# An earlier start for the feed-forward groups, two homes for their input, and an earlier switch of the cycle's form

## The chip, the core and the metric

The kernel runs on one core of one Trainium2 chip. Its engines work side by side and each takes its own instructions in order: TensorE (PE; its weight loads are shown apart as PEld), VectorE (DVE), ScalarE (ACT), GpSimd (POOL) and SyncE (SP), which issues the DMAs. The metric is the device time of one launch in microseconds, median of several runs; lower is better. TensorE's clock has two levels, 2.4 and 1.2 GHz; the profile shows the granted clock as 1.00 and 0.50.

## The reference

Attention over 64 heads (8 batches of 8 heads, 576 tokens, head size 64), in which scores more than tau below their row's maximum are dropped, and then a feed-forward layer over all 4608 tokens:

```python
scores = q @ k^T / sqrt(64)
thresh = max(scores) - tau
scores = where(scores >= thresh, scores, -1e9)
attn   = exp(scores - max) / (sum + 1e-9)
x = (attn @ v), heads side by side           # 4608 x 512
h = x @ w_in                                 # 512 x 2048
out = (max(h, 0) + alpha * min(h, 0)) @ w_out
```

## The kernel before

Two heads of a batch make a pair (32 pairs, 4 a batch, the class `Pair`). A pair has nine **units** (128 query rows of one head each, and one mixed unit at position 4). Most products are made from a high and a low part of each operand, three matmuls for one.

The main loop runs over **cycles** i from -3 to 297; unit i belongs to pair i // 9 at position i % 9, and the last unit is 287 (`total` = 288). The order of the instructions on TensorE, ScalarE, VectorE and GpSimd is the order in which this loop writes them down. In cycle i it masks unit i (L475, VectorE), makes the scores of unit i + 2 (L440, TensorE), turns unit i (L484 and L500, transposes on TensorE), then runs what tables hold for this cycle (`soon`, then `later`; `at_cycle` and `first_at_cycle` fill them), copies the turned unit (L536, ScalarE, high part; one cycle on L540, VectorE, low part) and takes a later unit's row maximum (L455, VectorE) and exponential with its threshold (L463 and L468, ScalarE). There are two score buffers, so scores of unit i + 2 wait for the mask of unit i.

The cycle has two **forms**. While i < SW (`ab`), maxima and exponentials are made two in each odd cycle and none in an even one, and the low part's place alternates; from SW on each cycle takes the low part of unit i - 1 right behind the scores and the maximum and exponential of unit i + 2 at its end. SW is 52.

The tables hold for each pair: products with v (L587) at positions 5, 6, 1 and 2, their copies out (L598, L600, ScalarE) one cycle on; the high part of the next pairs' keys `kh` (L367, ScalarE) and the low part `kl` (L374, GpSimd) at position 7; scaled queries (L387, L392) at position 0; and the pair's closing steps, the last of which (`fin_out`, L647) stores the pair's x (`xs`) to DRAM in position 7 of the next pair's turn. The first four pairs (one batch) are worked in whole 32-bit form and close one cycle later (cycle 44 for the batch).

The **feed-forward work** for the first seven of sixteen blocks of d_ff fills TensorE between attention's matmuls (class `Mlp`). Tokens go in 18 groups of 256. A group is ready RDY cycles behind the 36 units of the batch that holds its last token. For a group: `load_x` (one DMA, L206, into `xr`), `split_x` (xh on ScalarE, L212; xl on GpSimd, L214), seven chunks of layer 1 (`step_l1`, 12 matmuls each, L226), each followed by the activation (L238 VectorE, L239 ScalarE, L249 GpSimd) and its own split (L255, L256, GpSimd), then 42 matmuls of layer 2 (`step_l2`, L262), whose two sums are copied out by ScalarE (`po`, L768) and stored as `part`. `Mlp.cycle` holds a budget in assumed microseconds (`room`): each cycle adds CYCLE less what attention uses in it, a chunk costs 1.31 and a matmul of layer 2 costs 0.216; no chunk goes into the cycles with products with v, and at most GB = 11 chunks' results are kept. The x of a group stands in the same queue as its chunks, as an item of its own:

```python
if self.l1 and i >= self.gap and self.live < GB:
    if self.l1[0][2] is None:
        self.step_l1(i)          # load; split at i + XO; self.gap = i + XO + 2
    elif slot and self.room > TH1 and ...:
        l1 = True                # one chunk in this cycle
```

`xr`, `xh` and `xl` have one buffer each, so a group's x is loaded once the last chunk of the group before is out, and its first chunk follows three cycles later (XO = 1).

Behind the loop what is left of the queue is drained (`jobs`, `first_layer`, `second_layer`, x by `fetch_x`), and then the other nine blocks of d_ff are worked with a product scheme of seven multiplications (L1319 to L1612).

SyncE's DMAs are not in the hand-written order; the framework places them.

Of the kernel before, what the change touches and what calls it, by code (L numbers as in the profile page):

```python
# [11 lines left out]
F32R = mybir.dt.float32r  # L12
# [9 lines left out]
P = 128  # L22
D = 64
S = 576
NKC = 4
F1 = 7
G1 = 256
# [9 lines left out]
GB = 11  # L37
# [2 lines left out]
CLOSE = 10  # L40
DEC2, DEC3 = 5, 6
L2S = 7
SW = 52
THR = 'a'
QLV = 0
SPG = 'p'
# [4 lines left out]
FINS = (9, 11, 12, 12, 15, 16, 16)  # L51
ACTO, SPLO, PUTO = 1, 2, 1
TH1, TH2, TH3 = 0.75, -0.45, 0.1
XO = 1
L2O = 3
P1 = 2
LD = 12
# [3 lines left out]
EVD = lambda i: EVP[i % len(EVP)]  # L61
DEC0, DEC = -3, 3
DECO0, DECO = 16, 3
RDY = 13
CYCLE = 2.6
EW0, EW1, EW2 = (0, 1, 2, 3, 3, 3, 6), (0, 1, 2, 5, 6, 6, 7), (0, 1, 5, 6, 6, 7, 7)
EW = (
# [21 lines left out]
def tile_masked_attention_moe(  # L89
# [11 lines left out]
    nc = tc.nc  # L101
    B, NPAIR = q.shape[0], q.shape[1]
    NT, DM = out.shape
    NCC = DM // P
# [17 lines left out]
    groups1 = [(t, min(G1, NT - t)) for t in range(0, NT, G1)]  # L122
# [70 lines left out]
    ready = set()  # L193
# [504 lines left out]
    class Mlp:  # L698


        def __init__(self):
            self.l1, self.l2 = deque(), deque()
            self.acc = None
            self.live = 0
            self.gap = 0
            self.room = 0.0

        def ready(self, gi):
            t0, n = groups1[gi]
            st = {"g": {}}  # L710
            self.l1.append((gi, st, None))
            for i in range(F1):
                self.l1.append((gi, st, i))

        def step_l1(self, i):
            gi, st, fi = self.l1.popleft()
            t0, n = groups1[gi]
            if fi is None:
                st["xr"] = load_x(mem.mp1, t0, n, G1, 1)
                (at_cycle if i < total else first_at_cycle)(i + XO, lambda: st.update(x=split_x(mem.mp1, st["xr"], t0, n, G1, 1, nc.vector if i >= total else None)))  # L720
                self.gap = i + XO + 2
                return
            name = f"a{gi}_{fi}"
            self.live += 1
            ph = layer1(ps_m, fcs1[fi], n, st["x"], name)

            alone = i >= total

            def act(ph=ph):
                if alone:  # L730
                    st[fi] = (prelu(mem.mp1, G1, fcs1[fi], n, ph, name, 2),)
                    return
                st[fi] = prelu1(mem.mp1, G1, fcs1[fi], n, ph, name, 2)
                prelu2(*st[fi], n)

            def spl():
                g = mem.mp1.tile([P, 2, G1], F32R, tag="g", name=f"g{name}", bufs=GB)
                split_g(g, st.pop(fi)[0], n, None if alone else dict(p=nc.gpsimd, v=nc.vector).get(SPG))
                st["g"][fi] = g

            if alone:
                first_at_cycle(i + ACTO, act)
                first_at_cycle(i + SPLO, spl)
            else:
                at_cycle(i + ACTO, act)
                at_cycle(i + SPLO, spl)
            if fi == F1 - 1:
                for o in range(0, n, P):
                    for fj in range(F1):
                        self.l2.extend((i + L2O, gi, st, o, fj, ti) for ti in range(3))  # L750
# [22 lines left out]
        def cycle(self, i, used, slot):  # L773

            self.room = min(self.room, TH3) + CYCLE - used
            l1 = False
            if self.l1 and i >= self.gap and self.live < GB:
                if self.l1[0][2] is None:
                    self.step_l1(i)
                elif slot and self.room > TH1 and ("i", fcs1[self.l1[0][2]]) in ready:  # L780
                    l1 = True
                    self.room -= 1.31
            while self.l2 and self.l2[0][0] <= i and self.l2[0][4] in self.l2[0][2]["g"] and ("o", fcs1[self.l2[0][4]]) in ready and self.room > TH2:
                self.step_l2(i)
                self.room -= 0.216
            return l1
# [104 lines left out]
    def fetch_x(t0, n, c, lead, name, home):  # L891

        st = {}

        def load(k):
            if k == 0:
                st["parts"] = tuple(home.tile([P, NCC, G1], F32R, tag=t, name=f"{t}{name}", bufs=1) for t in ("xh", "xl"))
            xl = f(st["parts"][1])
            t = t0
            while t < t0 + n:  # L900
                b, o = divmod(t, S)
                m = min(S - o, t0 + n - t)
                nc.sync.dma_start(xl[:, k, t - t0 : t - t0 + m], xs[b][k, :, o : o + m])
                t += m

        def split(k):
            xh, xl = st["parts"]
            nc.scalar.activation(xh[:, k, :n], f(xl[:, k, :n]), AF.Copy)
            nc.gpsimd.tensor_tensor(xl[:, k, :n], f(xl[:, k, :n]), f(xh[:, k, :n]), op=ALU.subtract)
            if k == NCC - 1:  # L910
                st["x"] = st["parts"]

        for k in range(NCC):
            at_cycle(c, load, k)
            at_cycle(c + lead + k // 2, split, k)
        return st
# [4 lines left out]
    with tc.manual_schedule(engines=ENGINES) if ENGINES else ExitStack():  # L921
# [12 lines left out]
        for i in range(-3, total + CLOSE):  # L934
# [14 lines left out]
                do(i + 1, "expo")  # L949
            do(i, "turn")  # L950
            do(i, "turn_k")
            while nready < len(groups1) and sum(groups1[nready]) <= (i - RDY) // (9 * NPAIR) * S:
                mlp.ready(nready)
                nready += 1
            used = 0.92
# [747 lines left out]
```

## Time and profile before

| | |
|---|---|
| median of 3 runs | 1350.35 us (1349.82 to 1351.16) |
| profiled execution | 1351.17 us, its span 1349.4 us |
| mean granted clock of TensorE | 0.994 |
| busy | PE 1303.7 us, DVE 1133.0, ACT 957.9, POOL 773.3 |
| chain that ended last | PE 79%, DVE 8%, ACT 6%, DMA 3% |

The span is the time from the first to the last instruction; the rest of an execution's time lies around it. A row of a stretch gives the busy time of each engine in it, with the number of instructions; matmuls' ends are modelled, so a run of matmuls shows about 0.2 us more busy time than their starts lie apart. "Idle before" is the time for which an engine stood still ahead of an instruction, with what ended it.

### The profile page before, as it was taken

What the parts mean: (1) busy time and instruction counts of PE and PEld (TensorE: products, weight loads), DVE (VectorE), ACT (ScalarE), POOL (GpSimd) and SP (SyncE); (2) the same over time, 40 slices, a digit from 0 to 9 for tenths busy, and PEclk for the clock granted to TensorE, in tenths of its full rate; (3) what the DMA queues carried; (4) which work ended last, traced back from release to release, by engine and by line L of the source; (5) the groups of instructions that cost most, each with busy time, mean ns of one, the idle gap of its engine ahead of it and who ended that gap; (6) DMA issues with size and microseconds to landing.
All of it is one profiled execution on the core that took longest, in us unless ns stands there. A gap on an engine that the chain in (4) does not pass through costs nothing.

```text
span 1349.4 us, 26387 instructions
## 1 busy us (share of the span) xinstructions
PE 1303.7 (97%) x9052; PEld 1224.2 (91%) x9052; DVE 1133.0 (84%) x2150; ACT 957.9 (71%) x2103; POOL 773.3 (57%) x945
## 2 busy tenths in 40 slices
PE   5998899999999999999999999999999999999999
PEld 4556789999999999999999999889999999999999
DVE  6999888888888888988988987686788877977876
ACT  6888888888888888888888886254666666433332
POOL 4887476676576576666666654485888875000000
PEclk9999899999999999999999999999999999999999
DMA  8654544544554544454544533722566437766641
GB/s 258 165 153 115 150 128 113 162 132 121 148 142 125 141 138 136 135 140 136 141 134 136 139 89 112 248 66 87 186 191 188 161 109 254 247 197 190 201 134 70
DMA packets 140006, 202.98 MB, mean 150 GB/s; under 512 B 16000, under 2 KB 84640, under 8 KB 139872
## 3 DMA queue, kind: packets, MB, share of 16 engines
q1 hardware_dynamic: 139872, 201.29, 50.6%
q8 instruction: 72, 1.18, 0.4%
q14 instruction: 62, 0.51, 0.1%
HBM read 108.08 MB, written 51.00 MB: 118 GB/s over the span
## 4 chain that ended last, share of the span: by engine, by line
PE 79%; DVE 8%; ACT 6%; DMA 3%; issue 2%; POOL 1%; SPq 1%; ACTq 0%; DVEq 0%; POOLq 0%
PE av L587 11%; PE s L440 11%; PE pha L226 10%; PE acca L262 9%; PE t L484 8%; PE pX L1576 7%; PE pX L1319 6%; PE pW L1576 4%; PE pW L1319 3%; PE pY L1576 2%; PE pO L1337 2%; PE pY L1319 1%; PE accj L262 1%; DVE p L475 1%; PE tk L500 1%
## 5 line engine op out<-in xcount | busy, mean ns | idle before, releaser
L455 DVE TENSOR_REDUCE nmx<-s 128x1 f32<-128x576 f32 x288 | 217.3, 754 | 73.5 <-PE s L440 70.3
L475 DVE SCALAR_TENSOR_TENSOR p<-s,thr,p 128x576 f32<-128x576 f32 x256 | 207.0, 809 | 2.8 <-ACT thr L468 2.4
L463 ACT ACTIVATE p<-s,nmx 128x576 f32<-128x576 f32 x256 | 190.2, 743 | 6.6 <-DVE nmx L455 6.3
L262 PE MATMUL acca<-wo,ga 128*128 128x512 f32 x588 | 186.1, 423 | 0.8 <-issue 0.8
L440 PE MATMUL s<-kh,qst 128*128 128x288 f32 x640 | 142.1, 312 | 33.9 <-DVE p L475 21.1
L226 PE MATMUL pha<-xh,wi 128*128 128x256 f32 x792 | 158.5, 283 | 0.2 <-ACT pra L239 0.2
L484 PE MATMUL t<-ident,p 128*128 128x128 f32 x1024 | 155.1, 274 | 0.0
L440 PEld LDWEIGHTS s<-kh,qst 128*128 128x128 f32 x640 | 101.1, 192 | 57.5 <-issue 28.3
L440 PE MATMUL s<-kl,qst 128*128 128x288 f32 x640 | 134.2, 300 | 0.0
L226 PEld LDWEIGHTS pha<-xh,wi 128*128 128x128 f32 x792 | 129.0, 190 | 4.7 <-ACT pra L239 1.8
L484 PEld LDWEIGHTS t<-ident,p 128*128 128x128 f32 x1024 | 127.2, 142 | 0.1
L262 PEld LDWEIGHTS acca<-wo,ga 128*128 128x128 f32 x588 | 102.0, 191 | 12.5 <-issue 1.2
L226 PE MATMUL pha<-xl,wi 128*128 128x256 f32 x396 | 111.7, 282 | 1.3 <-DVE xl L214 1.3
L249 POOL TENSOR_TENSOR pta<-pta,pra 128x256 f32<-128x256 f32 x94 | 69.3, 737 | 74.0 <-ACT pra L239 69.8
L1319 PE MATMUL pX<-xh,wa 128*128 128x384 f32 x384 | 106.4, 337 | 1.0 <-DVE pZ L1392 0.5
L587 PE MATMUL av<-eo,vst 128*128 128x322 f32 (+1 forms) x512 | 107.3, 333 | 0.0
L540 DVE TENSOR_TENSOR eo<-t,eo 128x512 fp32r<-128x512 f32 (+1 forms) x168 | 97.4, 592 | 8.3 <-ACT eo L536 8.2
L440 PEld LDWEIGHTS s<-kl,qst 128*128 128x128 f32 x640 | 102.7, 192 | 0.0
L886 ACT ACTIVATE gh<-gr 128x1024 fp32r<-128x1024 f32 x45 | 47.7, 1060 | 76.8 <-PE pX L1576 32.5
L1576 PE MATMUL pX<-wb,gh 128*128 128x256 f32 x560 | 101.5, 283 | 0.0
L536 ACT ACTIVATE eo<-t 128x512 fp32r<-128x512 f32 (+1 forms) x168 | 84.6, 521 | 5.1 <-PE t L484 4.3
L1576 PEld LDWEIGHTS pX<-wb,gh 128*128 128x128 f32 x560 | 87.1, 191 | 0.0
(250 smaller groups left out, 3906.4 us busy)
## 6 DMA issues: line engine op xcount, KB each, us to landing
gd<-c SPq DMA_DIRECT2D x72, 192.0 KB
gr<-gd SPq DMA_DIRECT2D x24, 512.0 KB
kr<-in_k_dram SPq DMA_DIRECT2D x31, 320.0 KB
rb<-rvd SPq DMA_DIRECT2D x64, 144.0 KB
xs<-xa SPq DMA_DIRECT2D x32, 288.0 KB
pin<-part SPq DMA_DIRECT2D x18, 512.0 KB
vr<-in_v_dram SPq DMA_DIRECT2D x28, 320.0 KB
qr<-in_q_dram SPq DMA_DIRECT2D x31, 288.0 KB
```

Source lines behind the costliest of these rows:

```text
L226: nc.tensor.matmul(ph[:, :n], w[:, c, :], xx[:, c, :n], start=(c == 0 and ti == 0), stop=(c == NCC - 1 and ti == 2),)
L262: nc.tensor.matmul(acc[:m, :], gg[:, g, o : o + m], w, start=(first and ti == 0), stop=(last and ti == 2))
L440: nc.tensor.matmul(ps[:, h, :288], w, kk[:, a + h * 288 : a + (h + 1) * 288], start=(ki == 0 and i == 0), stop=(ki == 1 and i == n - 1),)
L455: nc.vector.tensor_reduce(self.nmx[:, j : j + 1], self.S[u][0][:, :, :288], axis=AX.XY, op=ALU.max, negate=True)
L463: nc.scalar.activation(pj, ps[:, :, :288], AF.Exp, bias=nmx[:, j : j + 1], scale=1.0)
L475: nc.vector.scalar_tensor_tensor(pj, ps[:, :, :288], thr[:, j : j + 1], pj, op0=ALU.is_ge, op1=ALU.mult, accum_out=self.sm[:, c : c + 1])
L484: nc.tensor.transpose(tb[:, c, :], pt[:, j, j * D + c * P : j * D + (c + 1) * P], ident)
L536: nc.scalar.activation(dst[0], ps, AF.Copy)
L540: nc.vector.tensor_tensor(dst[1], ps, f(dst[0]), op=ALU.subtract)
L587: nc.tensor.matmul(pa[:m, :n], w, x, start=(part == 0 and c == 0), stop=(part == z.parts[-1] and c == NKC))
L1319: nc.tensor.matmul(ph[:, :H1], a, x[:, c], start=(fresh and c == 0 and ti == 0), stop=(c == 1 and ti == 2), skip_group_check=not fresh,)
L1576: nc.tensor.matmul(acc[:, tb * H2 : (tb + 1) * H2], g[:, pr, tb * P : (tb + 1) * P], w, start=(fresh and (pr if final else n) == 0 and ti ...
```

## The change

- SW goes from 52 to 44: cycles 44 to 51 have the later form.
- RDY goes from 13 to 9: a group is ready four cycles sooner. Groups are no longer made ready behind the last unit.
- A group's x leaves the queue of chunks and gets a queue of its own (`xq`, `step_x`). It is loaded when at most XL = 2 chunks of the groups with a loaded x are left; its split follows XO = 2 cycles later (it was 1), and its chunks may go from the fourth cycle after the load on (`at`).
- `xh` and `xl` get two buffers each in the pool of the loop (also where `fetch_x` uses that pool).

```diff
@@ -40,7 +40,7 @@
 CLOSE = 10
 DEC2, DEC3 = 5, 6
 L2S = 7
-SW = 52
+SW = 44
 THR = 'a'
 QLV = 0
 SPG = 'p'
@@ -51,7 +51,8 @@
 FINS = (9, 11, 12, 12, 15, 16, 16)
 ACTO, SPLO, PUTO = 1, 2, 1
 TH1, TH2, TH3 = 0.75, -0.45, 0.1
-XO = 1
+XO = 2
+XL = 2
 L2O = 3
 P1 = 2
 LD = 12
@@ -61,7 +62,7 @@
 EVD = lambda i: EVP[i % len(EVP)]
 DEC0, DEC = -3, 3
 DECO0, DECO = 16, 3
-RDY = 13
+RDY = 9
 CYCLE = 2.6
 EW0, EW1, EW2 = (0, 1, 2, 3, 3, 3, 6), (0, 1, 2, 5, 6, 6, 7), (0, 1, 5, 6, 6, 7, 7)
 EW = (
@@ -699,27 +700,28 @@
 
 
         def __init__(self):
-            self.l1, self.l2 = deque(), deque()
+            self.l1, self.l2, self.xq = deque(), deque(), deque()
             self.acc = None
             self.live = 0
-            self.gap = 0
             self.room = 0.0
 
         def ready(self, gi):
             t0, n = groups1[gi]
             st = {"g": {}}
-            self.l1.append((gi, st, None))
+            self.xq.append((gi, st))
             for i in range(F1):
                 self.l1.append((gi, st, i))
+
+        def step_x(self, i):
+            gi, st = self.xq.popleft()
+            t0, n = groups1[gi]
+            st["xr"] = load_x(mem.mp1, t0, n, G1, 1)
+            (at_cycle if i < total else first_at_cycle)(i + XO, lambda: st.update(x=split_x(mem.mp1, st["xr"], t0, n, G1, 2, nc.vector if i >= total else None)))
+            st["at"] = i + XO + 2
 
         def step_l1(self, i):
             gi, st, fi = self.l1.popleft()
             t0, n = groups1[gi]
-            if fi is None:
-                st["xr"] = load_x(mem.mp1, t0, n, G1, 1)
-                (at_cycle if i < total else first_at_cycle)(i + XO, lambda: st.update(x=split_x(mem.mp1, st["xr"], t0, n, G1, 1, nc.vector if i >= total else None)))
-                self.gap = i + XO + 2
-                return
             name = f"a{gi}_{fi}"
             self.live += 1
             ph = layer1(ps_m, fcs1[fi], n, st["x"], name)
@@ -774,10 +776,10 @@
 
             self.room = min(self.room, TH3) + CYCLE - used
             l1 = False
-            if self.l1 and i >= self.gap and self.live < GB:
-                if self.l1[0][2] is None:
-                    self.step_l1(i)
-                elif slot and self.room > TH1 and ("i", fcs1[self.l1[0][2]]) in ready:
+            if self.xq and len(self.l1) - F1 * len(self.xq) <= XL:
+                self.step_x(i)
+            if self.l1 and i >= self.l1[0][1].get("at", i + 1) and self.live < GB:
+                if slot and self.room > TH1 and ("i", fcs1[self.l1[0][2]]) in ready:
                     l1 = True
                     self.room -= 1.31
             while self.l2 and self.l2[0][0] <= i and self.l2[0][4] in self.l2[0][2]["g"] and ("o", fcs1[self.l2[0][4]]) in ready and self.room > TH2:
@@ -894,7 +896,7 @@
 
         def load(k):
             if k == 0:
-                st["parts"] = tuple(home.tile([P, NCC, G1], F32R, tag=t, name=f"{t}{name}", bufs=1) for t in ("xh", "xl"))
+                st["parts"] = tuple(home.tile([P, NCC, G1], F32R, tag=t, name=f"{t}{name}", bufs=2 if home is mem.mp1 else 1) for t in ("xh", "xl"))
             xl = f(st["parts"][1])
             t = t0
             while t < t0 + n:
@@ -949,7 +951,7 @@
                 do(i + 1, "expo")
             do(i, "turn")
             do(i, "turn_k")
-            while nready < len(groups1) and sum(groups1[nready]) <= (i - RDY) // (9 * NPAIR) * S:
+            while i < total and nready < len(groups1) and sum(groups1[nready]) <= (i - RDY) // (9 * NPAIR) * S:
                 mlp.ready(nready)
                 nready += 1
             used = 0.92
```

## Rows read from the trace of the kernel before

**Rows 1.** The page, first part: busy time of an engine, share of the span, instructions.

```profile
PE 1303.7 (97%) x9052; PEld 1224.2 (91%) x9052; DVE 1133.0 (84%) x2150; ACT 957.9 (71%) x2103; POOL 773.3 (57%) x945
```

**Rows 2.** Stretches from the start of cycle 52 to that of 122 and on to 830 us. Columns here and in all rows of stretches: start:end and length in us; busy us (instructions) of PE, PEld, DVE, ACT, POOL; granted TensorE clock; share of the DMA engines; GB/s.

```profile
161.20:357.78 196.58, 193.15 (x1417) 183.65 (x1416) 173.81 (x387) 168.97 (x405) 129.83 (x166) 1.00 0.50 136
357.78:830.00 472.22, 470.96 (x3438) 448.35 (x3437) 414.50 (x918) 405.13 (x962) 307.73 (x388) 1.00 0.48 134
```

**Rows 3.** The chain that ended last, 900 to 925 us: start, length, what. Six chunks of layer 1 and 42 matmuls of layer 2.

```profile
904.15 8.82 PE phj L226 x72
912.98 9.52 PE accj L262 x42
```

**Rows 4.** Stretches of cycles 44, 45, 46, 47, of 48 to 51 together, and of 50 alone.

```profile
137.10:139.17 2.07, 1.31 (x9) 1.10 (x10) 1.66 (x4) 1.79 (x5) 2.07 (x3) 1.00 0.60 133
139.17:142.31 3.14, 1.20 (x8) 1.00 (x9) 2.96 (x8) 2.53 (x6) 0.73 (x2) 0.89 0.84 191
142.31:146.61 4.30, 4.30 (x20) 4.28 (x21) 3.17 (x6) 2.57 (x7) 1.19 (x1) 0.50 0.88 239
146.61:150.46 3.85, 3.85 (x24) 3.79 (x24) 1.75 (x4) 2.07 (x5) 0.00 (x0) 0.76 0.91 237
...
150.46:161.20 10.74, 8.82 (x58) 8.52 (x56) 9.11 (x22) 9.62 (x25) 7.26 (x8) 0.84 0.26 69
...
154.86:158.55 3.69, 3.69 (x19) 3.67 (x20) 3.10 (x8) 3.34 (x7) 2.47 (x2) 0.56 0.48 144
```

**Rows 5.** Stretches of cycles 54, 55, 56, of 57 to 60 together, of 59, and of 63, 64, 65.

```profile
166.36:169.58 3.22, 2.66 (x20) 2.48 (x21) 3.19 (x9) 3.13 (x8) 2.03 (x4) 1.00 0.92 263
169.58:171.93 2.35, 2.35 (x19) 2.28 (x20) 2.35 (x6) 1.56 (x5) 2.27 (x4) 1.00 0.64 169
171.93:175.05 3.12, 3.12 (x25) 3.06 (x24) 2.50 (x6) 2.65 (x7) 1.69 (x3) 1.00 0.74 189
...
175.05:185.59 10.54, 10.11 (x81) 9.88 (x80) 9.75 (x24) 9.18 (x26) 8.50 (x13) 1.00 0.22 58
...
180.18:182.94 2.76, 2.33 (x21) 2.12 (x19) 2.75 (x9) 2.03 (x6) 2.68 (x4) 1.00 0.29 70
...
190.75:194.04 3.29, 1.23 (x8) 1.02 (x9) 3.26 (x9) 3.20 (x8) 2.08 (x4) 1.00 0.92 263
194.04:196.48 2.44, 2.44 (x20) 2.31 (x20) 2.10 (x6) 2.22 (x5) 2.36 (x4) 1.00 0.69 172
196.48:200.03 3.55, 3.55 (x27) 3.40 (x26) 2.75 (x6) 2.66 (x7) 2.12 (x1) 1.00 0.67 167
```

**Rows 6.** Stretches of cycles 80 and 81.

```profile
239.44:242.22 2.78, 2.78 (x24) 2.68 (x23) 2.78 (x7) 2.37 (x8) 2.13 (x4) 1.00 0.89 235
242.22:245.05 2.83, 2.83 (x19) 2.46 (x17) 2.79 (x8) 2.74 (x7) 1.57 (x3) 1.00 0.88 255
```

**Rows 7.** ScalarE's timeline in cycle 205 (position 7): start, length, engine, line, operation, out<-in. `kh` of a coming pair, the turned unit's high part, and the exponential of the unit two on.

```profile
592.62 0.74 ACT L367 ACTIVATE kh<-kr 128x640 fp32r<-128x640 f32 x1
593.39 0.60 ACT L536 ACTIVATE eo<-t 128x512 fp32r<-128x512 f32 x1
593.88 0.73 ACT L463 ACTIVATE p<-s,nmx 128x576 f32<-128x576 f32 x1
```

**Rows 8.** The timelines of VectorE and TensorE behind it: low part, max, mask with the reading of its sum, and the scores that wait for the mask; then the same end of a mask and the scores behind it in cycle 210.

```profile
594.02 0.69 DVE L540 TENSOR_TENSOR eo<-t,eo 128x512 fp32r<-128x512 f32 x1 [0.27 <-ACT eo L536]
...
595.12 0.76 DVE L455 TENSOR_REDUCE nmx<-s 128x1 f32<-128x576 f32 x1
595.80 0.81 DVE L475 SCALAR_TENSOR_TENSOR p<-s,thr,p 128x576 f32<-128x576 f32 x1
596.53 0.08 DVE L475 DVE_READ_ACCUMULATOR p<-s,thr,p 128x1 f32 x1
...
597.13 0.42 PE L440 MATMUL s<-kh,qst 128*128 128x288 f32 x2
...
605.41 0.08 DVE L475 DVE_READ_ACCUMULATOR p<-s,thr,p 128x1 f32 x1
...
605.75 0.51 PE L440 MATMUL s<-kh,qst 128*128 128x288 f32 x2
```

**Rows 9.** The split of x on ScalarE (all 15; ns min/median/max), and stretches of three cycles with the same work at position 3: 201 without a split in the cycle before, 210 and 138 with one.

```profile
L212 ACT ACTIVATE xh<-xr x15: 1047/1061/1066, 155.7 to 842.2; 128x1024 fp32r<-128x1024 f32 x15
...
580.50:583.15 2.65, 2.65 (x17) 2.27 (x16) 2.18 (x6) 2.41 (x7) 1.20 (x5) 1.00 0.27 96
605.75:608.61 2.86, 2.77 (x17) 2.27 (x16) 2.44 (x6) 2.70 (x8) 2.54 (x6) 1.00 0.02 6
402.94:406.17 3.23, 2.78 (x18) 2.32 (x17) 2.97 (x6) 3.19 (x10) 2.91 (x6) 1.00 0.41 149
```

**Rows 10.** TensorE's timeline behind the loop: the two waits.

```profile
846.99 0.39 PE L226 MATMUL pha<-xl,wi 128*128 128x256 f32 x1 [1.25 <-DVE xl L214]
...
856.86 0.39 PE L226 MATMUL phj<-xh,wi 128*128 128x256 f32 x1 [2.08 <-ACT po L768]
```

**Rows 11.** SyncE's queue: the store of the last pair of the first batch, and the load of group 0's x; and, from the chain, a later load of x.

```profile
140.54 0.53 SPq L647 DMA_DIRECT2D xs<-xa  x1
...
143.29 0.38 SPq L206 DMA_DIRECT2D xr<-xs  x1
...
867.86 5.72 DMA xlj<-xs
```

## The prediction

> **What bounds the kernel now.** I read the page's first part: TensorE is busy 97% of the span, VectorE 84%, ScalarE 71% [rows 1]. Then the stretches. From 161.2 us on, TensorE stands still for only 196.58 - 193.15 = 3.4 us up to 357.8 and 1.3 us from there to 830 [rows 2]. In that part a cycle lasts as long as its matmuls, so moving matmuls between cycles gains nothing; only idle TensorE time can be won or lost. Third, the chain: six chunks of layer 1 take 8.82 us, 1.47 each; 42 matmuls of layer 2 take 9.52 us, 0.227 each [rows 3]. Last I cut the timeline at the first score matmul of each unit, which gives the cycles. Cycles 44 to 51 (no feed-forward work yet) take 24.1 us with TensorE idle for much of it and its clock at the lower level, 1.2 GHz, for parts [rows 4]; cycle 63 has 1.23 us of work in 3.29 [rows 5].
>
> **What the planner will do.** The planner's budget is plain arithmetic on cycle numbers, so both schedules can be walked through from the code. The old one then gives exactly the groups of L226 and L262 matmuls that the trace shows in each cycle. Old: chunks of group 0 in cycles 52, 53, 54, 57, 58, 61, 62; x of group 1 loaded in 63; its chunks in 66, 67, 70, 71, 76, 79, 80. New: 49, 52, 53, 54, 57, 58, 61, then without a gap 62, 63, 66, 67, 72, 76, 79. But group 2 needs the second batch and is ready only in cycle 81, so in 80 only one matmul of layer 2 is left and in 81 nothing. When the loop ends, the old plan has done 99 chunks and 567 matmuls of layer 2, the new one 100 and 561: 1.47 - 6 x 0.227 = 0.1 us. So the change moves work, and its effect is the change of idle time, place by place:
>
> 1. Cycles 44 to 51. Cycles 44 and 45 hold the same few matmuls in either form; after 1.20 us of work in 3.14 us the clock fell to 0.50 [rows 4], and I expect that again, so 44 to 47 stay as long. Cycles 48 to 51 take 10.74 us now [rows 4]. In the later form, the same positions of the next pair take 10.54 us with two chunks [rows 5]; the new plan has one chunk, in 49, and without the other between 9.1 and 10.54 us. I take 10.2: 0.5 us shorter with 1.47 us more work, so 2.0 us less idle. Bounds: 0 (the max in each cycle delays the mask behind it and eats all) and 4.7 (the low clock behind 141.6 us, 2.7 us by item 4, goes as well).
> 2. Cycles 63 to 65 become like 54 to 56: a chunk in 63 (3.22 us), five matmuls of layer 2 in 64 (2.35 + 1.13), then 3.12, together 9.8 us against 3.29 + 2.44 + 3.55 = 9.28 now [rows 5]. They hold one chunk and three matmuls more, 2.15 us; idle falls by 1.6 us.
> 3. Cycles 80 and 81 take 5.6 us now, full [rows 6]. The new plan leaves some 2.3 us of work there (cycles 44 and 45 show 1.31 and 1.20 us busy [rows 4], 0.2 us less each without the modelled end of the last matmul, and 0.23 for layer 2). In cycle 81 VectorE needs what it needs at the same position in cycle 45, 2.96 us [rows 4]; in cycle 80 scores, max and mask, one after the other, need 0.7 + 0.76 + 0.81 = 2.3 us [rows 8]. Of these 5.2 us 2.9 are idle. This gives back most of 1 and 2.
> 4. After those two cycles the clock can fall as it did at 141.6 us. For it: 0.96 us of work in 2.8 us, like the row at 139.17. Against it: cycle 63, 1.23 us in 3.29, did not lower it [rows 4, 5]. The fall at 155 us made cycle 50 3.69 us long against 2.76 at the same position in cycle 59, 0.9 us; the one at 141.6 us made 46 and 47 4.30 + 3.85 = 8.15 us long against 2.35 + 3.12 in 55 and 56, 2.7 us [rows 4, 5]. I take 1.7 us for one behind cycle 81, at even chances 0.8 us (bounds 0 and 2.7).
> 5. Where ScalarE splits x. The split (L212) is one instruction of 1.06 us [rows 9]. Now, in the loop, it falls on position (cycle mod 9) 5 four times, on 1 once and on 2 nine times; the plan puts it on 7 in cycles 97, 133, 169, 187 and 205, on 6 in cycle 60, on 2 four times, on 1 in cycles 244, 262 and 280. At position 7 ScalarE has no gap: kh, eo, p follow one another, and VectorE already waits 0.27 us for that eo [rows 7, 8]. The split goes in behind kh; queued behind it are eo, the exponential p and thr of a later unit. The eo then comes 1.06 us later, VectorE's subtraction with it, and its max and mask follow without slack. TensorE's next scores start 0.52 us after the mask's end; where TensorE waits for the mask, 0.26 us is the least [rows 8]. So 0.26 us are absorbed and 0.8 us lost, five times: 4.0 us. Bounds: 0 if lag elsewhere hides it, 1.06 each. At position 2 the split costs 2.86 - 2.65 = 0.21 us, and 0.58 in cycle 138 [rows 9]; the old nine cost some 2.7 us (seven like the first, two like the second). New: 4.0 + 4 x 0.3 + 0.4 (position 6, half of 7) + 3 x 0.1 (position 1: cycle 64, which has a split, against 55, 2.44 - 2.35 [rows 5]) = 5.9; net 3.2 us more, bounds -0.8 and 4.5. The subtraction on GpSimd (busy 57% [rows 1]) moves too; I cost it at nothing, since chunks start two cycles later; if it came late, the first chunk would wait for xl, as once behind the loop, 1.25 us [rows 10].
> 6. The end of the loop. Group 14's x is split one cycle earlier and into a second home, so TensorE's wait of 1.25 us for xl goes; but one more chunk stands on VectorE ahead of the copy po for which TensorE waits 2.08 us [rows 10], which may make that one longer. I take -0.3 us, bounds -2 and 1.5.
>
> The loads themselves win nothing: SP runs ahead, and group 0's x was issued at 143.29 us, as soon as xs, issued at 140.54, had landed [rows 11]. A second home costs no instruction.
>
> Sum: -2.0 - 1.6 + 2.9 + 0.8 + 3.2 - 0.3 = +3.0 us. The profiled execution took 1351.17 us (span 1349.4), which would be 1354.2; the median of the three runs is 0.8 lower, 1350.35, so **1353.4 us**.
>
> One rule speaks for the change throughout: the Trainium skill, page "Trainium Kernel Development and Optimization", section Best Practices, says to double-buffer so that DMA and compute overlap. By it every change of group should gain its gap. The rows differ: behind cycle 66 the gaps are filled with layer 2 and next to nothing is idle there [rows 2].
>
> **The rivals.**
> - A, the forecast: the split at position 7 costs 0.5 to 1.06 us each time. Sum with the other terms +1.5 to +4.3, and up to +6.2 with item 4 at its bound: 1351.8 to 1356.5 us. Chance 0.50, three quarters of it above +2.7 us.
> - B, ScalarE's lag is absorbed and a split at 7 costs 0.2 as at 2. For it: VectorE is often 0.5 us ahead. Item 5 falls to about 0.2: sum 0.0, 1350.4 us. Chance 0.27.
> - C, faster: the later form keeps the clock up at 141.6 us. It decides if the scores of units 46 to 48 come sooner than now; against it, cycles 44 and 45 get no work, and none is added before 49. Then item 1 gives -4.7, and the work behind reaches cycle 80 2.7 us sooner and may miss the fall of item 4. With B's price: -4.7 - 1.6 + 2.9 + 0 + 0.2 - 0.3 = -3.5, 1346.9 us. Chance 0.16.
> - D, a wait replaces the gap: x is not there when ScalarE comes to the split in cycles 47, 83, 119 or 155, right behind a batch's end. Issued at 143.29; such a load took up to 5.7 us [rows 11]; cycle 47 began at 146.61 [rows 4], so up to 2.4 us each time, four times; at half of that 4.8 us above A, 1358.2 us. Chance 0.05; it decides if ScalarE idles ahead of L212.
> - E, double-buffering pays as the rule has it: all of the 4.7 us idle behind 161.2 us [rows 2] go, 1345.6 us. Chance 0.02.
>
> **The numbers.** 0.2% (2.7 us) is about what a measurement of this kernel can tell from no change. Slower: 0.50 x 0.75 + 0.05 = 0.43. Same: 0.50 x 0.25 + 0.27 = 0.39. Faster: 0.18. The likeliest is A, whose own range is 1351.8 to 1356.5; the range for 8 in 10 takes in B and most of C and leaves out D's and E's ends: 1347 to 1357 us.
>
> **What would show it.** First L226 matmul in cycle 49, near 153.5 us, and no lower clock near 155 to 159; a chunk in 63; an idle stretch of 2 to 3 us near 240 us with the clock perhaps low behind it; L212 at position 7 of five pairs, and TensorE waiting 0.5 to 1 us for L475 one or two cycles on, where rows of before show none. Wrong if those five show no wait (B), if the clock stays high at 142 us (C), or if L212 waits for a DMA (D).

## The result, and the profile after

The changed kernel takes 1367.73 us (median of four runs, 1364.77 to 1368.26), the kernel before 1350.09 in the same comparison: 1.0126 times as long, 95% interval 1.0108 to 1.0143, or 17.6 us more. Forecast were 1353.4 us and a range of 1347 to 1357. The sign was the likeliest one, the size six times too small.

The page of after, first part, answers [rows 1]. The span is 1365.1 us, against 1349.4.

```profile
PE 1307.9 (96%) x9052; PEld 1223.5 (90%) x9052; DVE 1132.6 (83%) x2150; ACT 955.5 (70%) x2103; POOL 774.2 (57%) x945
```

As many matmuls, and 4 us more busy time for 16 us more span: TensorE stands still. Where it does, the starts of the same cycles in both traces tell (us, computed from the first score matmul of each cycle):

| | before | after | later | in this part |
|---|---|---|---|---|
| cycle 44 | 137.10 | 138.56 | 1.5 | +1.5 |
| cycle 52 | 161.20 | 163.16 | 2.0 | +0.5 |
| cycle 66 | 200.03 | 202.86 | 2.8 | +0.9 |
| cycle 85 | 253.54 | 258.22 | 4.7 | +1.9 |
| cycle 284 | 813.84 | 822.96 | 9.1 | +4.4 |
| first layer-2 matmul of job 0 | 865.64 | 882.04 | 16.4 | +7.3 |
| end | 1349.4 | 1365.1 | 15.7 | -0.7 |

The largest part lies behind the loop. TensorE's waits there, 815 to 990 us: engine, line, what it waited for, us in total, times, longest. The first row answers the 2.08 us of [rows 10].

```profile
PE phj L227 <- ACT po L770: 10.1, 1, 10.1
PE phj L227 <- DVE ptj L246: 1.2, 2, 0.6
```

TensorE's wait of 1.25 us for `xl` [rows 10] has no row any more. What ScalarE, SyncE and TensorE do around the long wait (the timelines of these engines, one behind the other; start, length, engine, line, operation, and in brackets the idle time before with what ended it); the last two lines are the same two copies on ScalarE in the kernel before:

```profile
865.30 0.42 ACT L254 ACTIVATE ga<-pta 128x256 fp32r<-128x256 f32 x1 [2.83 <-DVE pta L246]
865.62 0.58 ACT L770 ACTIVATE po<-acca 128x512 f32<-128x512 f32 x1
873.20 0.60 ACT L770 ACTIVATE po<-acca 128x512 f32<-128x512 f32 x1 [7.00 <-DMA part<-po]
...
864.27 1.83 SPq L1006 DMA_DIRECT2D w<-wid  x4
866.15 0.43 SPq L138 DMA_DIRECT2D wri<-in_moe_w_in_dram  x1
866.68 0.45 SPq L771 DMA_DIRECT2D part<-po  x1
867.17 6.26 SPq L905 DMA_DIRECT2D xlj<-xs  x8
...
873.85 0.58 PE L227 MATMUL phj<-xh,wi 128*128 128x256 f32 x1 [10.08 <-ACT po L770]
...
845.71 0.60 ACT L768 ACTIVATE po<-acca 128x512 f32<-128x512 f32 x1 [2.45 <-issue]
...
856.23 0.58 ACT L768 ACTIVATE po<-acca 128x512 f32<-128x512 f32 x1
```

The last two sums of the loop are copied out one behind the other. `po` has one home, so the second copy waits until the store of the first has landed. That store is issued at 866.68, behind four loads of 256 KB (`w`) and one of 512 KB (`wri`), and lands 6.4 us later. TensorE's next chunk waits for the second copy and stands. In the kernel before the two copies began at 845.71 and 856.23 us, and the first one's store had landed at 848.3.

The wait has a tail. Behind it TensorE's clock was granted at its lower level until 879.2 us, and the four chunks up to job 0 took 8.2 us, where four take 5.9 by [rows 3]. Stretches around the wait, after and before:

```profile
860.00:880.00 20.00, 9.78 (x52) 8.92 (x51) 7.30 (x19) 3.78 (x8) 2.93 (x4) 0.74 0.78 249
...
851.00:871.00 20.00, 17.92 (x107) 16.41 (x106) 14.58 (x31) 6.49 (x16) 7.65 (x10) 0.91 0.82 259
```

In the kernel before the clock fell behind the 2.08 us too, but for a shorter time: its five chunks took 8.8 us for 7.35. So the +7.3 us of the table are about 8.0 of longer wait and 0.9 of lower clock, less the wait for `xl`.

The second place is cycle 48. Stretches of cycles 48 to 50 of after (columns as in [rows 2]):

```profile
149.06:154.20 5.14, 1.54 (x11) 1.11 (x10) 2.14 (x5) 3.79 (x9) 2.63 (x3) 1.00 0.45 111
154.20:157.75 3.55, 3.55 (x21) 3.55 (x22) 3.32 (x9) 3.51 (x10) 3.32 (x5) 0.70 0.61 178
157.75:160.50 2.75, 2.75 (x20) 2.68 (x19) 2.07 (x6) 1.41 (x4) 1.61 (x3) 0.77 0.59 181
```

and the load of the first group's x in SyncE's queue and its split on ScalarE:

```profile
144.62 0.47 SPq L207 DMA_DIRECT2D xr<-xs  x1
...
150.35 1.06 ACT L213 ACTIVATE xh<-xr 128x1024 fp32r<-128x1024 f32 x1 [3.10 <-DMA xr<-xs]
```

ScalarE came to the split of the first group's x and stood 3.1 us for its load, which was issued at 144.62 us and landed 5.7 us later. The turned units, the maxima and TensorE stood behind it. TensorE had worked 1.54 us in the 5.14 of cycle 48, and the mean granted clock of cycle 49 is 0.70: part of it ran at the lower level. The +0.5 us of the table up to cycle 52 hide this. Cycles 44 to 47 took 10.5 us instead of 13.4, since the clock did not fall in 46; cycle 48 then took 5.1 instead of 1.1. Third, cycles 80 to 82, where [rows 6] show 80 and 81 full:

```profile
242.04:244.46 2.42, 1.48 (x13) 1.17 (x11) 2.42 (x6) 2.08 (x6) 1.78 (x3) 1.00 0.81 196
244.46:247.27 2.81, 1.23 (x9) 1.02 (x9) 2.65 (x8) 2.72 (x7) 1.43 (x3) 1.00 0.61 174
247.27:252.37 5.10, 5.10 (x25) 4.59 (x25) 3.05 (x6) 2.33 (x6) 0.96 (x1) 0.67 1.04 304
```

Fourth, the five splits at position 7. The first three of TensorE's waits from 286 to 620 us; the kernel before has none of them in the same cycles, its only row there is the last line:

```profile
PE tk L501 <- DVE eo L541: 1.3, 5, 0.4
PE pha L227 <- ACT pra L240: 1.0, 4, 0.2
PE av L588 <- DVE tt L541: 0.8, 1, 0.8
...
PE acca L262 <- issue: 0.8, 2, 0.4
```

and what stands behind the split of cycle 97 on ScalarE, VectorE and TensorE, with the stretch of cycle 98:

```profile
293.66 1.04 ACT L213 ACTIVATE xh<-xr 128x1024 fp32r<-128x1024 f32 x1
294.73 0.60 ACT L537 ACTIVATE eo<-t 128x512 fp32r<-128x512 f32 x1
...
295.36 0.69 DVE L541 TENSOR_TENSOR eo<-t,eo 128x512 fp32r<-128x512 f32 x1 [1.22 <-ACT eo L537]
...
296.10 0.33 PE L501 MATMUL tk<-ident,p 128*128 128x128 f32 x1 [0.42 <-DVE eo L541]
...
294.54:298.44 3.90, 3.48 (x25) 2.79 (x24) 3.08 (x7) 3.54 (x10) 3.89 (x3) 1.00 0.84 229
```

Five waits for `eo`, one for each split. The waits that have rows are less than what is lost. Cycle 98 took 2.75 us before and has one matmul of layer 2 more now, 0.23 us, so 0.93 us are lost in its 3.90; the row counts part of that as busy. By the starts of its matmuls some 0.6 of the 0.93 lie ahead of `tk`, and the rest at the chunk that follows. Worked out in the same way (length less the number of matmuls by their usual spacing, after less before) the five lose 0.93, 0.76, 0.91, 0.98 and 0.91 us, 4.5 in all.

The 1.5 us ahead of cycle 44 are not the change's: the order of the matmuls is the same there, and in the seventh run below, which has the whole change, cycle 44 begins at 136.16 us.

### The profile page after: what moved, and what is told of

It reads as the page before. It is cut to its first block, busy times and chain, and to the rows that moved or that the text cites. A ratio compares the mean times of both kernels' runs of the same rounds, so it can differ in the third digit from the quotient of the medians.

```text
span 1365.1 us, 26407 instructions
## 1 busy us (share of the span) xinstructions
PE 1307.9 (96%) x9052; PEld 1223.5 (90%) x9052; DVE 1132.6 (83%) x2150; ACT 955.5 (70%) x2103; POOL 774.2 (57%) x945
## 4 chain that ended last, share of the span: by engine, by line
PE 80%; DVE 8%; ACT 5%; issue 2%; POOL 2%; DMA 2%; SPq 1%; ACTq 0%; POOLq 0%; DVEq 0%
PE s L441 11%; PE av L588 11%; PE pha L227 10%; PE acca L263 9%; PE t L485 8%; PE pX L1578 7%; PE pX L1321 6%; PE pW L1578 4%; PE pW L1321 3%; PE pY L1578 2%; PE phj L227 2%; PE pY L1321 2%; PE pO L1339 2%; PE accj L263 1%; DVE p L476 1%
## 5 line engine op out<-in xcount | busy, mean ns | idle before, releaser
L227 PE MATMUL pha<-xh,wi 128*128 128x256 f32 x800 | 162.1, 286 | 1.2 <-ACT pra L240 1.2
```

The lines of the kernel that those rows point to most:

```text
L227: nc.tensor.matmul(ph[:, :n], w[:, c, :], xx[:, c, :n], start=(c == 0 and ti == 0), stop=(c == NCC - 1 and ti == 2),)
```

## The experiments

Each was compared with the kernel before on the same chip; ratios carry 95% intervals. The first four take the suspects one at a time.

### Two homes for the copy po

```diff
-po = mem.mp1.tile([P, DM], F32, tag="po", name=f"po{gi}_{o}", bufs=1)
+po = mem.mp1.tile([P, DM], F32, tag="po", name=f"po{gi}_{o}", bufs=2)
```

and the same for the jobs' `po` in that pool.

> The changed kernel with one thing more: the copy po of a finished layer-2 sum has two homes instead of one. Theory T: behind the loop the last two sums are copied out one after the other; the second copy waits until the first one's store has landed (866.68 to 873.09 us), and TensorE waits for it 10.1 us. With a second home the second copy can follow the first at about 866.3 us, so TensorE waits about 3 us instead of 10.1, and the kernel takes about 1360.5 us (1359 to 1362.5) instead of 1367.7. Rival: the transfers are what is late, and the wait moves to the next thing they bring (x of the next job, the weights), or to VectorE's decoding; then TensorE waits as long at another place and the time stays at 1366 to 1369 us.

Measured: 1358.05 us (1.0069, 1.0043 to 1.0095), 9.7 us less than the changed kernel and 1 us under the theory's range. The two copies now follow one another at once, and TensorE's wait is 3.0 us (ScalarE's timeline):

```profile
868.16 1.06 ACT L770 ACTIVATE po<-acca 128x512 f32<-128x512 f32 x2
```

(waits of TensorE behind the loop)

```profile
PE phj L227 <- ACT po L770: 3.0, 1, 3.0
```

From cycle 284 to the first layer-2 matmul of job 0 it takes 51.1 us, against 59.1 in the changed kernel and 51.8 before. The theory holds; what is left of the wait is VectorE's decoding ahead of the gate `ga`, as before. Of the 8.0 us between 59.1 and 51.1, 7.1 are wait; the rest is the clock, which fell behind this wait too, but for less: the four chunks took 7.3 us instead of 8.2.

### x loaded when one chunk is left

```diff
-XL = 2
+XL = 1
```

> The changed kernel, but a group's x is loaded when one chunk of the last group is left (XL = 1) instead of two. Walking through the planner's budget, the split of x then falls on position 7 of the pair once (cycle 61) instead of five times (97, 133, 169, 187, 205), and the loop leaves six chunks and 21 matmuls of layer 2 behind, like the kernel before, not five and 27. Theory: each split at position 7 costs 0.9 us (five: 4.5 us), and the order in which the old kernel empties its queue has no long wait for a copy po (7.3 us less behind the loop): about 1356 us (1354 to 1358). What stays is the idle stretch at cycles 81 and 82. Rival: the loss comes with loading early and with the second home as such, wherever the split falls: 1364 us or more.

Measured: 1353.92 us (1.0032, 1.0018 to 1.0047), at the theory's lower end. Behind cycle 84 no cycle loses the 0.9 us any more, and from cycle 284 to job 0 it takes 50.4 us. So the loss is not that of the early load and the second home as such, but of where the split falls and in what order the queue empties. The wait at cycle 48 stays (ScalarE stands 3.8 us there), and so does an idle stretch in cycle 81.

### The later form alone

```diff
-SW = 52
+SW = 44
```

on the kernel before.

> The kernel before with one line of the change alone: the later form of cycle from 44 (SW = 44). In the trace of the changed kernel cycles 44 to 47 lost 3.3 us less idle time than before, and cycle 48 lost 4.0 us more. Theory: the form only moves the stretch at the lower clock from cycle 46 to cycle 48, and the gain is what cycle 49's chunk fills: 0 to -1 us, 1349 to 1350.5 us. Rival: the form alone keeps the clock up and gives 2.5 to 4.7 us: 1345.5 to 1347.5 us.

Measured: 1349.30 us (0.9994, 0.9983 to 1.0006): no change that can be told. The trace first seems to speak for the rival: the clock stayed up in cycles 46 and 47, where [rows 4] show 0.50. But it fell in 64 and 65 instead, and so it did in the fifth run below, which has the old form (stretches of cycles 46, 47, 64 and 65 of that fifth run):

```profile
144.93:147.26 2.33, 2.33 (x19) 2.33 (x20) 2.00 (x4) 1.75 (x5) 1.18 (x1) 1.00 0.91 245
147.26:150.27 3.01, 3.01 (x25) 2.96 (x24) 2.72 (x7) 2.73 (x6) 0.00 (x0) 1.00 0.96 278
192.97:196.12 3.15, 3.15 (x19) 3.15 (x20) 2.74 (x6) 2.70 (x6) 3.07 (x4) 0.70 0.66 160
196.12:200.29 4.17, 4.17 (x26) 4.03 (x26) 2.09 (x4) 2.17 (x5) 1.39 (x1) 0.81 0.58 149
```

From cycle 44 to 66 the later form takes 60.7 us here and the old one 60.6 there. Where between cycles 44 and 66 the clock falls differs from run to run, and one trace doesn't show what the form does to it. Over all the traces here the clock was low in cycle 46 in one of three with the old form and in none of eleven with the later one; that is too few to tell, but where the clock fell at the same place, as in these two, the form made no difference.

### The first group sooner alone

```diff
-RDY = 13
+RDY = 9
-            while nready < len(groups1) and ...
+            while i < total and nready < len(groups1) and ...
```

on the kernel before.

> The kernel before with the first group four cycles sooner alone (RDY = 9, and groups made ready only while the loop runs, so that the same groups are left for behind it). By the planner's arithmetic the first chunk is in cycle 48, the splits fall on positions 0, 1 and 2 and once on 6 (cycle 60), and what is left behind the loop is as before. Theory: 1 us won at cycles 44 to 52, 1 us at 61 to 65, and 4 to 5 us lost where the feed-forward work of the first batch runs out ahead of cycle 81: about 1353 us (1351 to 1355). Rival: being sooner is what costs the 17 us: over 1360 us.

Measured: 1356.58 us (1.0052, 1.0035 to 1.0069), above the range of the theory and below that of the rival. The row of its splits shows what the theory had left out (idle time of ScalarE ahead of them: us, times):

```profile
  DMA xr<-xs: 7.7, 3
```

One of the three stands makes cycle 47 9.3 us long; and the work ran out in cycles 98 and 99 (3.5 us idle), not ahead of 81. Being sooner brings a wait for x.

### What a split costs at each position

```diff
+if i + 1 in (146, 154, 187, 196, 198, 213, 222, 233, 242, 255, 274, 266):
+    at_cycle(i + 1, lambda: nc.scalar.activation(idle_hi, idle_x, AF.Copy))
```

on the kernel before.

> The kernel before with twelve idle copies on ScalarE, each of the size of a split of x (128 x 1024 to fp32r), put where a split would stand in its cycle, at every position of the pair: cycles 198 (position 0), 154 (1), 146 (2), 255 (3), 274 (4), 266 (5), 213 and 222 (6), 187 and 196 (7), 233 and 242 (8). Nothing else is moved, so the cycle behind each shows its price. Theory: a price by position, 0.75 to 1.0 us at 7, about 1.1 at 6, at most 0.3 at 0, 1, 4 and 5, 0.2 to 0.6 at 2; together some 5 us, about 1355 us. Rival: ScalarE's lag is absorbed wherever it is and the changed kernel's 0.9 us at these cycles come from the moved matmuls: 0.2 us everywhere, 1352.5 us or less.

Measured: 1353.48 us (1.0028, 1.0017 to 1.0039). The lines are cycles 199, 155 and 256 (behind copies at positions 0, 1 and 3), 224 (two cycles behind the copy at position 6), 197 (behind position 7) and 233 itself (position 8):

```profile
577.16:580.12 2.96, 2.96 (x23) 2.56 (x22) 2.83 (x7) 2.62 (x8) 2.88 (x5) 1.00 0.28 87
451.50:454.51 3.01, 3.01 (x25) 2.96 (x24) 2.04 (x5) 2.68 (x7) 0.00 (x0) 1.00 0.25 73
739.72:742.43 2.71, 2.71 (x18) 2.40 (x16) 2.48 (x7) 2.67 (x9) 1.94 (x2) 1.00 0.34 100
648.26:651.56 3.30, 3.06 (x25) 2.68 (x23) 3.08 (x7) 2.96 (x9) 2.56 (x4) 1.00 0.76 203
570.62:574.30 3.68, 3.21 (x24) 2.66 (x23) 3.07 (x7) 3.34 (x9) 2.00 (x4) 1.00 0.86 236
674.27:677.48 3.21, 3.01 (x25) 2.69 (x23) 3.15 (x9) 3.21 (x9) 1.99 (x4) 1.00 0.90 243
```

In the kernel before they are 2.74, 3.01, 2.70, 2.74, 2.75 and 2.74 us long. So one copy costs 0.2 us at 0, nothing at 1 and 3, 0.56 at 6, 0.93 at 7 and 0.47 at 8; the others gave 0.18 at 2, nothing at 4 and 5, and 0.92, 0.53 and 0.49 at the second 7, 6 and 8. The twelve sum to 4.3 us, the medians differ by 4.4. ScalarE's lag has a price of its own, by position; at 6 the theory had twice too much. The six dear copies, those at 6, 7 and 8, are all paid for in the cycle at position 8, the one in which the changed kernel lost its five times 0.9 us.

### The good parts together

The changed kernel with

```diff
-XO = 2
-XL = 2
+XO = 1
+XL = 1
-RDY = 9
+RDY = 13
```

and two homes for `po`.

> What the runs so far speak for, together: the changed kernel with RDY = 13 (the first group no sooner), XO = 1 and XL = 1, so that by the planner's arithmetic chunks stand in the cycles of the kernel before and the splits fall on positions 0, 1 and 5 alone, the later form from 44, two homes for x and two for po. Theory: the later form gives 2.3 us net between cycles 43 and 66 as in the trace of the run with that form alone, nine splits at 1 instead of 2 some 2 us, TensorE's wait for xl behind the loop (1.3 us) goes: about 1345 us (1343.5 to 1347.5). Rival: the form's gain is given back behind cycle 63 and the copies po wait behind VectorE's decoding: 1348.5 to 1350.5 us.

Measured: 1349.97 us (1.0007, 0.9997 to 1.0017): the rival. Cycle 284 begins 3.8 us sooner than before, and the wait behind the loop takes it back:

```profile
PE phj L227 <- ACT po L770: 5.0, 1, 5.0
```

(ScalarE's timeline)

```profile
853.51 0.42 ACT L254 ACTIVATE ga<-pta 128x256 fp32r<-128x256 f32 x1 [2.81 <-DVE pta L246]
853.83 1.07 ACT L770 ACTIVATE po<-acca 128x512 f32<-128x512 f32 x2
```

Both copies stand on ScalarE behind a gate that waits for VectorE's decoding: the same wait, for another reason. The clock was low behind it again, from 853.6 to 860.5 us.

### Weights loaded later

On the changed kernel, with one home for `po`:

```diff
         for _ in range(PUTO + 1):
             cycle()
+        fetch_w32(0)
+        fetch_w32(1)
```

(both calls taken from ahead of the drain).

> The changed kernel, with the four loads of decoded weights (w<-wid, 256 KB each) issued behind the last copies po instead of ahead of them; one home for po as in the changed kernel. In its trace they go out at 864.27 to 866.15 us, and the store of the first copy, issued at 866.68, takes 6.4 us to land. Theory: the store is slow because these transfers are still running; without them it lands 2 to 3 us after its issue, TensorE waits about 6 us instead of 10.1, 1362 to 1364.5 us. Rival: the loads of x issued right behind the store are what slows it, or the store's place in the queue: still about 10 us, 1366 to 1369 us.

Measured: 1361.15 us (1.0090, 1.0071 to 1.0108; two executions), 1 us under the theory's range. One of the four loads still went out ahead of the store, with the `wri` load of 512 KB, and three went behind it; the store, issued at 864.38, landed 3.3 us later, then the second copy began (ScalarE's timeline), and TensorE waited 6.5 us:

```profile
867.76 0.60 ACT L770 ACTIVATE po<-acca 128x512 f32<-128x512 f32 x1 [3.41 <-DMA part<-po]
```

3.3 us instead of 6.4: what else is in flight sets how long the one home is taken. The run doesn't part the loads ahead of the store from those behind it: the loads of x, which followed the store at once in the changed kernel, now follow 1.9 us later, behind the three of weights.

### The first group's x in time

On the changed kernel with two homes for `po`:

```diff
+            if i == 41:
+                mlp.x0 = load_x(mem.mp1, 0, G1, G1, 1, q)
```

and `step_x` takes `x0` for the first group.

> The changed kernel with two homes for po, and x of the first group alone loaded three to four cycles sooner, out of q instead of out of the attention's output, which isn't there yet (so the output of the first 256 rows is not the reference's). To be held against the run with two homes for po alone (1358.05 us). Theory: ScalarE stood 3.1 to 4.1 us ahead of the split in cycle 47 for the load, and TensorE with it in cycle 48; with x there in time cycle 48 takes 2.4 to 3 us instead of 5.1 to 6.1 and the clock stays at its upper level through cycle 50 as in the run with the later form alone: 3.5 to 5 us less, 1353 to 1354.5 us. Rival: the wait only uncovers a slack there was anyway, and the time is won at most in part: over 1356.5 us.

Measured: 1353.81 us (1.0040, 1.0025 to 1.0056), 4.2 us less than with the two homes alone. Its cycles 48 to 50:

```profile
147.16:149.52 2.36, 1.32 (x12) 1.08 (x10) 2.17 (x5) 2.32 (x8) 2.21 (x4) 1.00 0.27 63
149.52:152.13 2.61, 2.61 (x21) 2.61 (x22) 2.50 (x7) 2.58 (x9) 2.44 (x4) 1.00 0.54 152
152.13:154.83 2.70, 2.32 (x21) 2.12 (x19) 2.70 (x8) 2.10 (x6) 1.66 (x3) 1.00 0.70 201
```

What took 5.14, 3.55 and 2.75 us in the changed kernel takes 2.36, 2.61 and 2.70. The group could start in cycle 49, if only its x were there.

### Work held back for cycles 80 and 81

On the changed kernel with two homes for `po`:

```diff
-... and self.room > TH2:
+... and self.room > (0.6 if 70 <= i < 80 else TH2):
```

> The changed kernel with two homes for po, and layer 2 held back in cycles 70 to 79: a matmul of it is issued only while the planner's room is above 0.6 instead of -0.45. By its arithmetic a chunk and four matmuls then stand in cycle 80 and eight in 81, where the changed kernel has one and none; two splits instead of five fall on position 7. To be held against the run with two homes alone (1358.05 us). Theory: the first batch's feed-forward work ran out ahead of cycle 81, and the idle time there is filled out of cycles that have more than they need: 2.9 us at cycles 80 and 81, up to 3 us of the lower clock in 82, and three splits at 0.93 us each, 1350 to 1354 us. Rival: the idle time only moves into cycles 70 to 79, which lose what 80 to 82 gain; then the splits alone give 2.8 us: 1355 us or more.

Measured: 1352.98 us (1.0035, 1.0023 to 1.0047), 5.1 us less than with the two homes alone. Cycles 80 to 82:

```profile
240.69:244.19 3.50, 3.50 (x27) 3.28 (x26) 3.28 (x8) 3.16 (x9) 2.86 (x4) 1.00 0.75 204
244.19:247.01 2.82, 2.82 (x18) 2.48 (x17) 2.79 (x8) 2.57 (x6) 1.70 (x3) 1.00 0.65 153
247.01:249.30 2.29, 2.29 (x21) 2.23 (x19) 1.67 (x5) 1.60 (x4) 1.84 (x3) 1.00 1.02 264
```

There is no idle time and no fall of the clock. Held against the trace with the two homes alone, at equal work, cycles 70 to 75 lose 1.3 us, 80 and 81 win 2.9 and 82 wins 2.9 (in that trace the clock was low from 247.9 to 254.7 us, twice as long as in the changed kernel's). Three splits have left position 7.

### Three versions against the kernel before

The good parts, with `(XL if i < total else 0)` in place of `XL`:

> The run of the good parts together (RDY = 13, XO = 1, XL = 1, later form, two homes for x and po) with one thing changed: behind the loop the next x is loaded only when no chunk is left, so that six chunks and 21 matmuls of layer 2 are left over in the order of the kernel before, not five and 27. Theory: that run's loop ended 3.8 us sooner than in the kernel before, and the two copies po stacked up behind one decoded gate took it back (TensorE waited 5.0 us for po); with the old order behind the loop the time from cycle 284 to the first second-layer matmul of job 0 is 50.3 to 51.8 us instead of 54.6, and the kernel takes 1345 to 1347.5 us. Rival: the loop's 3.8 us were a matter of when the clock fell, and the time stays within 1348.5 to 1351 us.

The good parts, with the last gates five cycles later (`i + SPLO + (5 if i >= total + 8 else 0)`):

> The run of the good parts together, with the gates of the last two chunks (ScalarE's ga and GpSimd's remainder, which the second layer of job 0 needs only later) issued five cycles later, so that the copies po stand ahead of them on ScalarE. Theory: the two copies then go as soon as their sums are done, TensorE's wait of 5.0 us for po falls to under 1.5 us, and the kernel takes 1345 to 1347 us. Rival: VectorE's decoding holds up the next chunk's own gate (ptj) just as long and TensorE waits for that instead: 1348.5 to 1351 us.

And with both:

> The good parts together (RDY = 13, XO = 1, XL = 1, later form, two homes for x and po), with both ends: the next x loaded behind the loop only when no chunk is left, and the gates of the last chunk issued behind the copies po. Theory: each end alone took the wait for po from 5.0 to 2.1 and 0.7 us; both together leave under 1 us, and as VectorE's decoding is then next in line little more is won than by one of them: 1346 to 1347.5 us. Rival: the two add up, 1344 to 1345.5 us.

Measured: 1346.77 us (0.9989, 0.9977 to 1.0000), 1347.49 (0.9991, 0.9979 to 1.0002) and 1347.00 (0.9989, 0.9978 to 1.0000). The first and third lie within their theories, the second between theory and rival. In the first two traces TensorE waits for `po` 2.1 and 0.7 us, and the part from cycle 284 to job 0 takes 50.5 and 50.3 us instead of 54.6; part of that is the clock, which was not low behind these shorter waits. In the third TensorE doesn't wait for `po` at all and that part takes 48.1 us, but from there to the end it takes 483.7 us against 481.4 in the first trace: what the later gates win ahead of job 0 they lose behind it. All three lie about 2 us under the kernel before, at the edge of what can be told, and 20 us under the changed one.

## Why the prediction was wrong

The sign was right, but for the most part not for the reasons given: what cost most, the one home of `po` and the late x, is not in the sum. Each run held against the kernel before on its own chip, 9.5 us of the 17.6 are the one home of `po`, 3.4 the late x, and 4.3 the idle cycles 80 to 82 with three of the splits, together 17.2. The shares are rough: the interval of the first alone is 7 us wide, and the second and third were each measured with two homes for `po` but not together. What is left of gains and losses must about cancel.

- **Item 6 failed** (forecast -0.3, bounds -2 and 1.5; measured +7.3 between cycle 284 and job 0). It asked how much longer VectorE would keep the copy waiting, which was 2.08 us in [rows 10], and took that for the whole price. It didn't ask which buffer the copy writes, how many homes that has, and what stands ahead of its store in SyncE's queue. The row of before gave no hint, since there the store had landed long ago. Nor did it count the clock, which is low behind such a wait (some 0.9 us more than before). The part of the item that names a gain was right: the wait of 1.25 us for `xl` is gone.
- **Rival D came true in one of its four places**, with about the price given to it (up to 2.4 us; ScalarE stood 3.1 us, and with the fall of the clock behind it 3.4 to 4.2 us hang on it). Its chance of 0.05 was the mistake: by the prediction's own numbers a load issued at 143.29 that takes 5.7 us lands at 149.0, after the start of cycle 47 at 146.61. That was a forecast, not a remote case. In the trace of before the same load landed 6.3 us after its issue, at 149.5; nobody needed it until 155.7. It should have replaced item 1's gain.
- **Item 1** had cycles 44 to 47 stay as long, with the clock low in 46; it stayed up there, and they took 2.9 us less. Without the wait for x the item was right in kind: with x in time cycles 44 to 51 take 20.9 us instead of 24.1. How much of that is owed to the clock can't be said, since the old form shows 19.7 in the fifth run.
- **Item 2**: cycles 63 to 65 take 9.2 us (forecast 9.8, before 9.28). But the split in cycle 60 made cycle 61 1.1 us longer (forecast 0.4); the fifth run prices position 6 at about 0.55, and the rest is open.
- **Items 3 and 4 were right.** 3.0 us idle in cycles 80 and 81 (forecast 2.9), and a fall of the clock in 82 that cost 1.7 us (forecast 1.7 at even chances, so 0.8 in the sum). That the fall came was chance: it is there in three of the four traces with that gap, and not in the one with x in time.
- **Item 5 was right in size, wrong in place**: 4.5 us for five splits at position 7 (forecast 4.0). TensorE doesn't wait for the mask but one step sooner: the next `tk` is released by VectorE's `eo`, and that is what comes late. Rival B (absorbed) is ruled out by the fifth run. The list of splits lacked one, in cycle 226 at position 1, which the item prices at 0.1 us. Another 1.0 us was lost in cycle 109, behind eight matmuls of layer 2 in 108: there TensorE's products with v waited 0.8 us for VectorE's `tt` (the third row of waits above); why `tt` came so late is open.
- **Rivals C and E** didn't come as times. C's sign was there: the clock stayed up at 142 us. But a run with the old form shows that too, and the form alone gives no change of time that can be told. For E, no run has the second home for x alone; the good parts, which have it with the later form, are no faster than the kernel before. The rule of double-buffering (the Trainium skill, "Trainium Kernel Development and Optimization", section Best Practices: overlap DMA with compute) paid at another buffer: it was the store behind `po` that computing waited for, and a second home there won 9.7 us by medians.

## What to carry to other kernels

When a change moves the order in which a queue empties, list every buffer with a single home that the emptying writes, and for each the store that must land before it is free, with what stands ahead of it in the DMA queue; a wait of before doesn't price this if its store was early, and a long wait of TensorE can cost a stretch at the lower clock behind it as well. Where the work for a stretch is a fixed amount, starting sooner moves the idle time to the stretch's end unless some of it is held back, and a consumer moved sooner must be held against the landing time of its load. A step on a busy engine has a price by its place in the cycle (here 0 to 0.93 us for the same instruction), and one run with idle copies at every place measures them all.

## What was not expected of the hardware

- A store of 256 KB took 6.4 us from issue to landing with 1.5 MB of loads issued in the 2.4 us ahead of it, and 3.3 us with 0.75 MB in 2.0 us; two such stores earlier in the changed kernel's trace, issued at 838.64 and 846.52 us, landed 2.0 us later. The Trainium skill ("DMA: Bandwidth & Descriptors", section Anatomy of one DMA) gives a fixed part of about 2.0 us and a part by size, which makes 2.6 us for it (an estimate, from a fit to DMAs of another issuing path); the quiet stores take less, the one behind many loads more than twice that.
- TensorE's clock falls in other cycles from run to run of the same order of instructions: 0.50 in cycle 46 in the kernel before, 0.70 in cycle 64 in the fifth run; and the stretch of cycles 2 to 6 took 12.65 us at 0.87 before and 14.79 us at 0.77 after, with the same matmuls:

```profile
19.63:34.42 14.79, 12.14 (x57) 8.69 (x57) 12.34 (x24) 11.45 (x28) 8.65 (x12) 0.77 0.82 241
```

The Trainium skill ("TensorE: Matmul & The Clock Gate", part 1) says of the slow matmuls at a kernel's start that their number varies between runs of one kernel; these traces show the like for falls in the middle.

With that goes the spread of the times. Of the 18 executions of the kernel before beside the first four experiments the shortest took 1345.61 us at a mean granted clock of 0.999, the longest 1351.56 us at 0.995. An effect of 2 us can't be read from one execution.
